# A key load that waits for another load's products: GpSimd's second key transfer held behind w_gate's matmuls

## The chip, the cores and the metric

The kernel runs on one core of one Trainium2 chip. The metric is the device time of one execution in microseconds (us); the median of three runs is compared. All numbers are float32.

## The reference

Two branches read the same x (4 rows of 512) and are mixed by a gate for each row. Branch a is attention of one query per row over a cache of 4096 keys and values in 32 heads of 128; branch b is a gated feed-forward block with 1792 inner columns.

```python
g = sigmoid((x * gate_w).sum(-1, keepdims=True))
q = (x @ wq)                                   # 4 rows x 32 heads x 128
scores = einsum("bhqd,bhkd->bhqk", q, k_cache) * (128 ** -0.5)
a = einsum("bhqk,bhkd->bhqd", softmax(scores), v_cache) @ wo
b = (gelu(x @ w_gate) * (x @ w_up)) @ w_down
out = g * a + (1 - g) * b
```

The caches make up nearly all of the data: 4 x 32 x 4096 x 128 numbers each, 537 MB for the two together. The whole kernel reads 565 MB.

## The kernel before

*Tiles.* The attention runs over 32 tiles (NT). A tile is one row b of x and a group g of four heads, with all 4096 keys: 128 partitions (4 heads x 32), each with 128 keys of 128 numbers, 65,536 bytes to a partition, 8.4 MB for the keys of a tile and as much for its values. Tile i has b = i % 4 and g = i // 4.

*Work of a tile.* DVE multiplies the keys by the query, in place (`products`, L385), and sums over the 128 numbers (`sums`, L391), both in two parts: first the quarter of the tile that shares its place with the neighbouring tile's keys (`shared=True`, 4096 numbers a partition), then the other three quarters (12288). `soft_max` takes the maximum on DVE and the exponentials on ACT. PE multiplies the weights by the values (`pv`, L417), one tile behind. DVE's two big steps make up most of its time.

*Places.* All large operands lie in one on-chip tensor, `big`. Even and odd tiles' keys lie in two places that overlap by one quarter, so the load of key tile i+1 has to wait until DVE has summed the shared quarter of tile i. The values have one place (from `VA` on), so the load of value tile i waits for PE's `pv(i - 1)`. At the start the place of the values is used for other things: first wq, then w_gate (`F0`) and w_up (`F1`), whose places begin where wq lay, and the feed-forward's temporaries.

*Order.* A small planner (`Plan.add`) holds a list of steps. Each step names its engine, what it reads and what it writes, as ranges of named tensors; the planner derives the waits: a step waits for the last earlier step, on another engine, that touches an overlapping range, if one of the two writes it. Each engine runs its own steps in the order of the list. A name in these ranges need not be a tensor: a range of a made-up name makes one step wait for another in the same way. The middle tiles run as a loop over groups with the same steps; tile 0 and the end are written out.

*Loads.* `load` (L260) gives the first four large loads to SyncE's queue (SP): wq, key tile 0, w_gate and w_up. All later ones go to GpSimd's queue (POOL): key tile 1, value tile 0, key tile 2, value tile 1 and so on, in the order of the list. A load issued by GpSimd holds up the ones behind it in that queue while it waits. w_gate and w_up are issued when PE has finished with wq.

*The feed-forward at the start.* In tile 0, between DVE's products of the three quarters and their sums, the list has `gates()` (a tiny product on PE, an Exp on ACT and six small steps on DVE that give the gate), `ffn_up(0)` and `ffn_up(1)` (x times w_gate and x times w_up on PE, 32 matmuls each, L519, and a copy by ACT, L524), `ffn_gelu()` (five steps on DVE with a Tanh on ACT between, L531 to L536, and a transpose into hT, L538) and then the load of value tile 0. The gelu's temporaries lie in w_up's place, so it can begin only when w_up's products are done, and value tile 0's load waits for the last of these steps. The other half of the feed-forward, with w_down, is done at the end, together with the product with wo.

Of the kernel before, what the change touches and what calls it, by code (L numbers as in the profile page):

```python
# [132 lines left out]
def tile_gated_mix(tc: tile.TileContext, x, kc, vc, wq, wo, w_gate, w_up, w_down, gate_w, out):  # L133
# [4 lines left out]
    F = w_gate.shape[1]  # L138
    KC = DM // P
# [5 lines left out]
    NT = B * NG  # L145
    TW = R * D
# [22 lines left out]
    def sb(pool, name, shape):  # L169
        sizes[name] = math.prod(shape[1:])  # L170
        return pool(name, [P] + list(shape[1:]), F32).ap()[:shape[0]]
# [5 lines left out]
    xT = sb(head, "xT", [P, KC, 4, B, 8])  # L177
# [31 lines left out]
    q = sb(ps, "q", [P, B, D])  # L209
# [6 lines left out]
    Q0, F0, F1, W0, D0 = VA, VA, VA + KC * F, VA, VA + TW // 2  # L216
# [4 lines left out]
    def place(a, n):  # L221
        return big[:, a:a + n]

    def z(a, n):
        return ("big", a, a + n)

    def t(*names):
        return [(n, 0, sizes[n]) for n in names]
# [17 lines left out]
    def dve(emit, reads, writes):  # L246
        return add("dve", emit, reads, writes)

    def act(emit, reads, writes):
        return add("act", emit, reads, writes)  # L250

    def pe(emit, reads, writes):
        return add("pe", emit, reads, writes)
# [4 lines left out]
    def load(dst, src, writes, lane):  # L258
        e, queue = ("sp", nc.sync) if sum(x.engine == "sp" for x in plan.steps) < 4 else ("pool", G)
        return add(e, lambda: queue.dma_start(dst, src), (), writes, lane=lane if e == "sp" else "p" + lane, unit=16)  # L260

    def load_kv(kind, i):
        src = (vc, kc)[kind == "k"]
        a = KB_ * (i % 2) if kind == "k" else VA if i < NT - 1 else 0
        s = src[i % B, HT * (i // B):HT * (i // B) + HT].rearrange("h (p r) d -> (h p) (r d)", p=PH)
        load(place(a, TW), s, [z(a, TW)], "vl" if kind == "v" and i == NT - 1 else kind)

    def KA(i):
        return KB_ * (i % 2)
# [86 lines left out]
    def gates():  # L356
        pe(lambda: T.matmul(sm[:, :B], ones[:B], gd, start=True, stop=True), t("ones", "gd"), [("sm", 0, B)])
        act(lambda: A.activation(g4, sm[:, :B], AF.Exp, scale=-1.0), [("sm", 0, B)], t("g4"))
        dve(lambda: V.tensor_scalar(g4, g4, 1.0, None, op0=OP.add), t("g4"), t("g4"))
        dve(lambda: V.reciprocal(g4, g4), t("g4"), t("g4"))  # L360
        dve(lambda: V.tensor_tensor(g16.rearrange("p (j b) -> p j b", b=B), m16.rearrange("p (j b) -> p j b", b=B),
                                    g4[:, None, :].to_broadcast([P, 4, B]), op=OP.mult), t("m16", "g4"), t("g16"))
        dve(lambda: V.tensor_reduce(g1, g16, axis=AX.X, op=OP.add), t("g16"), t("g1"))
        dve(lambda: V.tensor_scalar(half, g1, -0.5, 0.5, op0=OP.mult, op1=OP.add), t("g1"), t("half"))
        dve(lambda: V.tensor_tensor(gmask, g4[:, :, None].to_broadcast([P, B, HT]),
                                    pmask[:, None, :].to_broadcast([P, B, HT]), op=OP.mult), t("g4", "pmask"), t("gmask"))

    def q_pick(g):
        dve(lambda: V.tensor_scalar(HC, hmask[:, bass.ds(row(g - 1) * HT + HT, HT), None].to_broadcast([P, HT, PH]), 1.0,  # L369
                                    None, op0=OP.mult), t("hmask"), t("hc"))  # L370
# [6 lines left out]
    def rows(i, shared):  # L377
        return ((R - RO, R), (0, R - RO))[not shared] if i % 2 == 0 else ((0, RO), (RO, R))[not shared]

    def products(i, shared):  # L380
        b = i % B
        r0, r1 = rows(i, shared)
        k = place(KA(i), TW).rearrange("p (r d) -> p r d", d=D)[:, r0:r1]
        m = [z(KA(i) + r0 * D, (r1 - r0) * D)]
        dve(lambda: V.tensor_tensor(k, k, QB[:, b:b + 1, :].to_broadcast([P, r1 - r0, D]), op=OP.mult),  # L385
            m + t("qb"), m)

    def sums(i, shared):
        r0, r1 = rows(i, shared)
        k = place(KA(i), TW).rearrange("p (r d) -> p r d", d=D)[:, r0:r1]  # L390
        dve(lambda: V.tensor_reduce(SC[i % 2][:, r0:r1], k, axis=AX.X, op=OP.add),  # L391
            [z(KA(i) + r0 * D, (r1 - r0) * D)], [(f"sc{i % 2}", r0, r1)])
# [17 lines left out]
    def pv(i):  # L410
        b, n = i % BP, i // BP % 2
        N, m = RJ * D, R // RJ

        def emit():
            for j in range(m):
                c, m0 = j % 4, PZ + 32 * j - RJ * HT * b
                last = T.matmul(PO[n][32 * c:32 * c + 32].rearrange("p j d -> p (j d)"), PM[:, m0:m0 + 32],  # L417
                                place(VAT(i) + j * N, N), start=b == 0 and j < 4, stop=b == BP - 1 and j >= m - 4)
            return last

        pe(emit, t("PM") + [z(VAT(i), TW)], t(f"po{n}"))

    def gather_a(i):
        n = i // BP % 2
        act(lambda: A.activation(O[n], PO[n], AF.Copy), t(f"po{n}"), t(f"o{n}"))  # L425

    def gather(g):
        N = B // BP

        def emit():  # L430
            for n in range(N):
                m0 = BP * HT * (1 - n)
                for j in range(RJ):
                    T.matmul(sm[:B * HT, :D], selv[:, j, m0:m0 + B * HT], O[n][:, j, :],  # L434
                             start=(n, j) == (0, 0), stop=(n, j) == (N - 1, RJ - 1))
            return T.matmul(sm[:B * HT, D:], RS.rearrange("p b h -> p (b h)"), ones[:, :1], start=True, stop=True)  # L436

        pe(emit, t("o0", "o1", "sel", "RS", "ones"), t("sm"))
# [52 lines left out]
    def attended(w, e):  # L491
        a, m = ES + w * E * 32 + e * 32, (W0, W1)[w] + e * DM
        return place(a, 32), place(m, DM), [z(a, 32), z(m, DM)]
# [21 lines left out]
    def ffn_up(s):  # L515
        def emit():
            for c in range(KC):
                for j in range(4):
                    last = T.matmul(q.rearrange("p b d -> p (b d)")[32 * j:32 * j + 32, :FG], xTf[:, c, :32],  # L519
                                    place((F0, F1)[s] + c * F + j * FG, FG), start=c == 0, stop=c == KC - 1)  # L520
            return last

        pe(emit, t("xT") + [z((F0, F1)[s], KC * F)], t("q"))
        act(lambda: A.activation(fu[:, s, :FG], q.rearrange("p b d -> p (b d)")[:, :FG], AF.Copy),  # L524
            t("q"), [z(FU + s * DM, FG)])

    def ffn_gelu():
        x1, r1 = fu[:, 0, :FG], [z(FU, FG)]
        (t1, z1), (t2, z2), (t3, z3), (th, z4), (y, z5), (v, z6) = (
            (place(F1 + a * DM, FG), [z(F1 + a * DM, FG)]) for a in range(6))  # L530
        dve(lambda: V.tensor_tensor(t1, x1, x1, op=OP.mult), r1, z1)  # L531
        dve(lambda: V.tensor_scalar(t2, t1, 0.044715, 1.0, op0=OP.mult, op1=OP.add), z1, z2)
        dve(lambda: V.tensor_tensor(t3, t2, x1, op=OP.mult), z2 + r1, z3)
        act(lambda: A.activation(th, t3, AF.Tanh, scale=c_gelu), z3, z4)
        dve(lambda: V.scalar_tensor_tensor(y, th, 1.0, x1, op0=OP.add, op1=OP.mult), z4 + r1, z5)  # L535
        dve(lambda: V.scalar_tensor_tensor(v, y, half, fu[:, 1, :FG], op0=OP.mult, op1=OP.mult),  # L536
            z5 + t("half") + [z(FU + DM, FG)], z6)
        dve(lambda: V.transpose(hT, v.rearrange("p (k i) -> p i k", i=FC)), z6, t("hT"))  # L538
# [10 lines left out]
    for i in range(NT):  # L549
        g, b = divmod(i, B)  # L550
        plan.turn = (i - 1) // B if 0 < i < NT - B + 1 else None
        if b == 1 and g + 1 < NG:
            q_pick(g + 1)
        products(i, True)
        sums(i, True)
        if i < NT - 1:
            load_kv("k", i + 1)
        else:
            load_kv("v", i)
        products(i, False)  # L560
        if i == 0:
            gates()
            ffn_up(0)
            ffn_up(1)
            ffn_gelu()
            load_kv("v", 0)
        sums(i, False)
        if i > 0:
            pv(i - 1)
            if i < NT - 1:  # L570
                load_kv("v", i)
            if i % BP == 0:
                gather_a(i - 1)
            if b == 0:
                gather(g - 1)
            if b == 3 and g + 1 < NG:
                q_spread()
        soft_max(i)
        if i > 0 and b == 0:
            weigh(g - 1)  # L580
# [25 lines left out]
    for h in range(2):  # L606
        for e in range(WO_END[1][-1], E):
            s, w, reads = attended(1, e)
# [52 lines left out]
```

## Time and profile before

| what | value |
|---|---|
| median of 3 runs | 1316.59 us (1316.15 to 1318.24) |
| the profiled execution | 1318.02 us, span 1316.6 us |
| mean granted TensorE clock | 0.638 |
| DVE busy | 1158.4 us, 88% of the span |
| PE busy | 354.3 us, 27% |
| ACT busy | 87.3 us, 7% |
| data over the span | 564.8 MB, mean 429 GB/s |
| w_gate's load, issue to landing | 18.2 us |
| w_up's load, issue to landing | 36.8 us |

The profile shows one execution. The span goes from the first to the last instruction; the execution's own time is 1.4 us longer. A row of the timeline gives the start, the duration, the engine with the line and the operation, what it writes and reads, and in brackets how long the engine stood idle before it and what ended that. DMA issues of GpSimd are rows of POOL. A row of a stretch of time gives the length, then each engine's busy time with its number of instructions, the granted clock, the mean busy share of the 16 DMA engines, and the GB/s moved. A packet is counted where it starts, so the share of a short stretch can be over 1.

### The profile page before, as it was taken

The page shows a single profiled execution, that of the slowest core. Times are in us where ns is not written, and L with a number is a line of the kernel's source. Part 1 is how long each engine was busy: PE and PEld are TensorE (multiplying, and loading weights), DVE is VectorE, ACT ScalarE, POOL GpSimd, SP SyncE. Part 2 cuts the span into 40 slices and gives each one's busy share as a digit, 9 for nine tenths or more (in the row PEclk, how much of TensorE's full clock was granted, in tenths as well). Part 3 has the DMA queues.
Part 4 walks back from the last instruction along what each step waited for, and adds up shares of the span by engine and source line. Part 5 has one row for each costly group of instructions (what it writes and reads, how often), then busy time and mean ns, then how long its engine had stood idle before and what let it go on. Part 6 is the DMA issues. An engine that isn't in the chain of part 4 may idle for free.

```text
span 1316.6 us, 6158 instructions
## 1 busy us (share of the span) xinstructions
PE 354.3 (27%) x2512; PEld 100.4 (8%) x2512; DVE 1158.4 (88%) x303; ACT 87.3 (7%) x291; POOL 38.8 (3%) x78
## 2 busy tenths in 40 slices
PE   3212222122332113322211222321133222122227
PEld 0000000000010000100000000100001000010002
DVE  1769999999999898999989899998989999998992
ACT  0000000000000000000000000000000000000001
POOL 0000000000000000000000000000000000000000
PEclk9556665666666566666556666655666665666668
DMA  9988999999999999999999999999999999999998
GB/s 415 443 354 383 445 432 431 442 418 442 440 424 442 434 430 442 424 436 442 422 442 434 430 442 424 436 446 418 442 440 424 442 430 434 442 418 441 438 427 370
DMA packets 10602, 564.83 MB, mean 429 GB/s; under 512 B 1232, under 2 KB 1240, under 8 KB 1504
## 3 DMA queue, kind: packets, MB, share of 16 engines
q0 software_dynamic: 9984, 540.55, 94.9%
q1 hardware_dynamic: 592, 24.13, 4.3%
q8 instruction: 7, 0.11, 0.0%
q14 instruction: 3, 0.02, 0.0%
q10 hardware_dynamic: 16, 0.02, 0.0%
HBM read 564.67 MB, written 0.01 MB: 429 GB/s over the span
## 4 chain that ended last, share of the span: by engine, by line
DMA 71%; DVE 26%; PE 2%; issue 1%; ACT 0%; SPq 0%; DVEq 0%
DMA big<-in_A_k_cache 65%; DVE sc L391 13%; DVE big L385 12%; DMA big<-in_B_w_up 3%; DMA big<-in_A_wo 2%; DMA big<-in_A_wq 2%; PE po L331 1%; PE q L519 0%; PE acc L506 0%; PE wide L498 0%; PE po L506 0%; DVE hT L538 0%; DVE big L536 0%; DVE big L531 0%; DVE big L535 0%
## 5 line engine op out<-in xcount | busy, mean ns | idle before, releaser
L385 DVE TENSOR_TENSOR big<-big,qb 128x4096 f32<-128x4096 f32 x64 | 555.9, 8687 | 86.9 <-DMA big<-in_A_k_cache 86.9
L391 DVE TENSOR_REDUCE sc<-big 128x32 f32<-128x4096 f32 x64 | 555.9, 8686 | 2.3
L417 PE MATMUL po<-big,PM 128*32 128x512 f32 x2048 | 293.8, 738 | 900.0 <-DMA big<-in_A_v_cache 900.0
L417 PEld LDWEIGHTS po<-big,PM 128*32 128x32 f32 x2048 | 72.2, 132 | 1115.7 <-DMA big<-in_A_v_cache 823.6
L403 ACT ACTIVATE PM<-sc,nb 32x128 f32<-32x128 f32 x128 | 67.2, 525 | 478.7 <-DVE nb L398 431.9
L425 ACT ACTIVATE o<-po 128x512 f32<-128x512 f32 x16 | 9.6, 597 | 443.0 <-PE po L417 443.0
L260 POOL DMA_DIRECT2D big<-in_A_v_cache x32 | 16.9, 528 | 607.6 <-PE po L417 560.4
L260 POOL DMA_DIRECT2D big<-in_A_k_cache x31 | 16.5, 532 | 613.2 <-DVE sc L391 613.2
L403 ACT ACTIVATION_READ_ACCUMULATOR PM<-sc,nb 32x1 f32 x128 | 26.1, 204 | 0.0
L375 ACT ACTIVATE qb<-q 128x512 f32<-128x512 f32 x8 | 4.8, 597 | 246.1 <-PE q L373 246.1
L519 PE MATMUL q<-big,xT 128*32 128x448 f32 x64 | 11.4, 883 | 25.3 <-DMA big<-in_B_w_up 13.7
L348 DVE TENSOR_TENSOR big<-po,amask 128x512 f32<-128x512 f32 x2 | 1.3, 686 | 19.0 <-PE po L331 19.0
L434 PE MATMUL sm<-o,sel 128*16 128x128 f32 x128 | 15.4, 273 | 5.8 <-ACT o L425 5.8
L331 PE MATMUL po<-big,xT 128*32 128x512 f32 x64 | 9.4, 755 | 19.1 <-DMA big<-in_A_wq 19.1
L434 PEld LDWEIGHTS sm<-o,sel 128*16 128x16 f32 x128 | 11.7, 97 | 14.4 <-ACT o L425 13.1
L616 DVE COPY res<-acc 4x144 f32<-4x144 f32 x1 | 0.3, 296 | 13.0 <-PE acc L506 13.0
L373 PE MATMUL q<-QM,hc 128*128 128x512 f32 x16 | 10.0, 707 | 4.2 <-DVE hc L369 4.2
L531 DVE TENSOR_TENSOR big<-big 128x448 f32<-128x448 f32 x1 | 0.6, 626 | 10.9 <-PE q L519 10.9
L396 DVE TENSOR_REDUCE m<-sc 128x1 f32<-128x128 f32 x32 | 9.2, 286 | 1.1
L441 DVE RECIPROCAL ri<-sm 16x1 f32<-16x1 f32 x8 | 1.2, 155 | 8.4 <-PE sm L436 8.4
L397 DVE STREAM_TRANSPOSE mt<-m 128x32 f32<-128x32 f32 x32 | 6.8, 212 | 1.1
L398 DVE TENSOR_REDUCE nb<-mt 128x1 f32<-128x32 f32 x32 | 5.9, 186 | 1.1
(78 smaller groups left out, 73.8 us busy)
## 6 DMA issues: line engine op xcount, KB each, us to landing
big<-in_A_wo POOLq DMA_DIRECT2D x1, 4096.0 KB, 28.2
big<-in_B_w_gate SPq DMA_DIRECT2D x1, 3584.0 KB, 18.2
big<-in_B_w_up SPq DMA_DIRECT2D x1, 3584.0 KB, 36.8
big<-in_B_w_down POOLq DMA_DIRECT2D x1, 3584.0 KB, 19.1
big<-in_A_wo POOLq DMA_DIRECT2D x1, 1792.0 KB, 26.3
big<-in_A_wo POOLq DMA_DIRECT2D x1, 1280.0 KB, 28.8
big<-in_A_v_cache POOLq DMA_DIRECT2D x32, 29.1
big<-in_A_wo POOLq DMA_DIRECT2D x1, 512.0 KB, 29.5
```

Source lines behind the costliest of these rows:

```text
L260: return add(e, lambda: queue.dma_start(dst, src), (), writes, lane=lane if e == "sp" else "p" + lane, unit=16)
L331: last = T.matmul(PO[s][32 * j:32 * j + 32].rearrange("p j d -> p (j d)"), xTf[:, c, :32], w[:, n0:n0 + HB * D], start=c == 0, stop=c == K ...
L373: pe(lambda: T.matmul(q.rearrange("p b d -> p (b d)"), HC.rearrange("p h k -> p (h k)"), QM.rearrange("p b d -> p (b d)"), start=True, sto ...
L385: dve(lambda: V.tensor_tensor(k, k, QB[:, b:b + 1, :].to_broadcast([P, r1 - r0, D]), op=OP.mult), m + t("qb"), m)
L391: dve(lambda: V.tensor_reduce(SC[i % 2][:, r0:r1], k, axis=AX.X, op=OP.add), [z(KA(i) + r0 * D, (r1 - r0) * D)], [(f"sc{i % 2}", r0, r1)])
L396: dve(lambda: V.tensor_reduce(M1[n], SC[n], axis=AX.X, op=OP.max), t(f"sc{n}"), t(f"m1{n}"))
L397: dve(lambda: V.transpose(MT, M1[n].to_broadcast([P, PH])), t(f"m1{n}"), t("mt"))
L403: last = A.activation(PM[:, PZ:].rearrange("p (c m) -> p c m", m=32)[s, :, h:RJ * HT:HT], SC[n][s, :].rearrange("p (c j) -> p c j", j=RJ), ...
L417: last = T.matmul(PO[n][32 * c:32 * c + 32].rearrange("p j d -> p (j d)"), PM[:, m0:m0 + 32], place(VAT(i) + j * N, N), start=b == 0 and j ...
L425: act(lambda: A.activation(O[n], PO[n], AF.Copy), t(f"po{n}"), t(f"o{n}"))
L434: T.matmul(sm[:B * HT, :D], selv[:, j, m0:m0 + B * HT], O[n][:, j, :], start=(n, j) == (0, 0), stop=(n, j) == (N - 1, RJ - 1))
L519: last = T.matmul(q.rearrange("p b d -> p (b d)")[32 * j:32 * j + 32, :FG], xTf[:, c, :32], place((F0, F1)[s] + c * F + j * FG, FG), start ...
```

## The change

The load of key tile 1, and no other, gets one more range, `("turn", 0, 1)`, which it is said to write. `ffn_up(s)` is said to read `("turn", s, s + 1)`, so `ffn_up(0)`, the products with w_gate, touches the same range. For the planner to see it first, the call of `ffn_up(0)` moves ahead of the load in the list, and with that ahead of DVE's `products(0, False)` and of `gates()`. As a result GpSimd waits for the last of w_gate's matmuls, besides DVE's sums of the shared quarter, before it issues key tile 1. PE now has w_gate's matmuls ahead of the gate's tiny product, and ACT has w_gate's copy ahead of the gate's Exp. DVE's own order is as before. The number of loads, their sizes, their queues and their order within each queue stay the same. `ffn_up(1)`'s range `("turn", 1, 2)` is touched by no other step.

```diff
@@ load_kv
-        load(place(a, TW), s, [z(a, TW)], "vl" if kind == "v" and i == NT - 1 else kind)
+        load(place(a, TW), s, [z(a, TW)] + [("turn", 0, 1)] * (kind == "k" and i == 1), "vl" if kind == "v" and i == NT - 1 else kind)
@@ ffn_up
-        pe(emit, t("xT") + [z((F0, F1)[s], KC * F)], t("q"))
+        pe(emit, t("xT") + [z((F0, F1)[s], KC * F), ("turn", s, s + 1)], t("q"))
@@ the loop over the tiles
         products(i, True)
         sums(i, True)
+        if i == 0:
+            ffn_up(0)
         if i < NT - 1:
             load_kv("k", i + 1)
         else:
...
         products(i, False)
         if i == 0:
             gates()
-            ffn_up(0)
             ffn_up(1)
             ffn_gelu()
             load_kv("v", 0)
```

## The prediction

> **What bounds the kernel now.** I read the page's DMA queues first, then the span cut into four stretches, then the timeline of the stretch that stood out, and last the start of three loads in tenths of a microsecond. In the queue rows the last figure is the time of the packets as a share of 16 engines' span. In the stretches the last three figures are the granted clock, the DMA share and GB/s.
>
> ```profile
> span 1316.6 us, 6158 instructions
> ...
> PE 354.3 (27%) x2512; PEld 100.4 (8%) x2512; DVE 1158.4 (88%) x303; ACT 87.3 (7%) x291; POOL 38.8 (3%) x78
> ...
> q0 software_dynamic: 9984, 540.55, 94.9%
> q1 hardware_dynamic: 592, 24.13, 4.3%
> ...
> 0.00:77.00 77.00, 24.02 (x136) 7.20 (x136) 33.11 (x38) 3.06 (x5) 1.36 (x7) 0.76 0.99 423
> 77.00:104.75 27.75, 1.74 (x12) 0.43 (x16) 26.83 (x12) 2.69 (x9) 1.06 (x2) 0.54 0.72 303
> 104.75:1310.00 1205.25, 324.34 (x2289) 90.33 (x2284) 1097.93 (x252) 80.44 (x274) 36.38 (x69) 0.63 1.00 434
> 1310.00:1316.60 6.60, 4.25 (x90) 2.41 (x83) 0.56 (x2) 1.14 (x3) 0.00 (x0) 1.00 0.42 169
> ```
>
> The two queues that carry the data fill 99.2% of the span. From 104.75 us to 1310 us the DMA share is 1.00, at 434 GB/s: one unbroken stream, and nothing done earlier by a compute engine can shorten it. The tail after 1310 us is the last products. The only hole is between 77 and 104.75 us: 0.28 x 27.75 us = 7.8 us in which no data moved. DMA is the bound, and what this kernel can win without moving fewer bytes is about 7.8 us. DVE, at 88% of the span, is second. In the hole it is busy nearly all the time (26.83 of 27.75 us), so it is DVE's order of work that left DMA without a load.
>
> ```profile
> 42.28 4.43 DVE L385 TENSOR_TENSOR big<-big,qb 128x4096 f32<-128x4096 f32 x1 [5.73 <-DMA big<-in_A_k_cache]
> 50.79 5.33 PE L519 MATMUL q<-big,xT 128*32 128x448 f32 x32 [11.59 <-DMA big<-in_B_w_gate]
> 51.08 12.95 DVE L385 TENSOR_TENSOR big<-big,qb 128x12288 f32<-128x12288 f32 x1
> 51.48 0.67 POOL L260 DMA_DIRECT2D big<-in_A_k_cache  x1 [48.28 <-DVE sc L391]
> 56.18 0.54 ACT L524 ACTIVATE big<-q 128x448 f32<-128x448 f32 x1 [16.77 <-PE q L519]
> 63.95 0.16 DVE L359 TENSOR_SCALAR g<-g 128x4 f32<-128x4 f32 x1
> ...
> 64.84 0.17 DVE L365 TENSOR_TENSOR gmask<-g,pmask 128x16 f32<-128x16 f32 x1
> 69.84 6.04 PE L519 MATMUL q<-big,xT 128*32 128x448 f32 x32 [13.72 <-DMA big<-in_B_w_up]
> 75.94 0.63 DVE L531 TENSOR_TENSOR big<-big 128x448 f32<-128x448 f32 x1 [10.94 <-PE q L519]
> ...
> 79.68 0.94 DVE L538 STREAM_TRANSPOSE hT<-big 128x448 f32<-128x448 f32 x1
> 80.54 12.91 DVE L391 TENSOR_REDUCE sc<-big 128x96 f32<-128x12288 f32 x1
> 80.93 0.53 POOL L260 DMA_DIRECT2D big<-in_A_v_cache  x1 [28.78 <-DVE hT L538]
> 94.42 4.42 DVE L385 TENSOR_TENSOR big<-big,qb 128x4096 f32<-128x4096 f32 x1
> 103.01 8.68 PE L417 MATMUL po<-big,PM 128*32 128x512 f32 x64 [27.13 <-DMA big<-in_A_v_cache]
> 103.59 0.53 POOL L260 DMA_DIRECT2D big<-in_A_k_cache  x1 [22.13 <-DVE sc L391]
> ...
> big<-in_B_w_gate SPq DMA_DIRECT2D x1, 3584.0 KB, 18.2
> big<-in_B_w_up SPq DMA_DIRECT2D x1, 3584.0 KB, 36.8
> ```
>
> The timeline's columns are start, duration, engine, line and operation; in brackets stands the idle time before it and what ended it. The last two rows are the page's DMA issues, with the time from issue to landing. The start reads like this. Key load 1 is issued at 51.48 us, as soon as DVE's sums of the first quarter free its place, while w_up, queued behind w_gate on SP, is still on its way. The two loads share the engines, so w_up is seen by PE only at 69.84 us, 19.05 us after w_gate, though both hold 3584 KB. DVE idles 10.94 us for w_up's products, does the gelu, and only its last step (hT) frees the place of value load 0, issued at 80.93 us. By then key load 1 is through: hole one. Because DVE is late, key load 2 too is issued late, at 103.59 us, after value load 0 has landed (PE starts on it at 103.01): hole two.
>
> **The change, part by part.** *The wait.* Key load 1 now also waits for the first group of L519, which ends at 50.79 + 5.33 = 56.12 us; with the 0.3 us that GpSimd takes after a release (hT ends at 80.62, its load is issued at 80.93) it goes out at 56.4, 4.9 us later than before. Behind it in GpSimd's queue stands only value load 0, which is due far later. Its reader, DVE's next tile, is due at 94.42 before and about 83.9 after (below).
>
> *w_up alone.* 3.67 MB at 434 GB/s are 8.5 us behind w_gate: PE sees it at 50.79 + 8.5 = 59.3 us instead of 69.84, and its last bytes move between about 58.2 and 59.2. L519's second group takes 6.04 us: 65.3. DVE's small steps for the gate end at 65.01 anyhow, so the gelu starts at 65.4 instead of 75.94: DVE is 10.5 us earlier. The gelu's chain (75.94 to 80.62) ends at 70.1.
>
> *ffn_up(0) ahead of the gate's product.* PE's tiny product for the gate, and ACT's Exp behind it, now stand behind w_gate's group and its copy:
>
> ```profile
> 38.62 0.59 PE L357 MATMUL sm<-gd,ones 4*128 4x4 f32 x2
> ...
> 39.24 0.17 ACT L358 ACTIVATE g<-sm 128x4 f32<-128x4 f32 x1
> ```
>
> They end near 57 us (56.72 for the copy, 0.17 for the Exp) and DVE wants the result at 63.95: 6.9 us of cover, cost nothing. Were the cover gone, the delay would fall on the gelu one for one.
>
> *Hole one.* Value load 0 goes out at 70.4. Key load 1 brings the same bytes behind the same bytes as before, so if the stream does not break around 58 us it ends where it ended, by 77 us. The next load then waits in the queue with 5 us to spare, and the hole is gone.
>
> *Hole two.* DVE's tile 1 moves from 94.42 to 83.9, key load 2 from 103.59 to 93.1, its first bytes to 94.3. Value load 0's bytes (128 partitions of 65,536 bytes, 8.39 MB, 19.3 us at 434 GB/s) now follow at once on key load 1's, from 77.2, 4.9 us sooner than the 82.1 of the row below, and end near 96.5: 2.2 us to spare, hole gone. Value load 1 waits for PE's products on value load 0 (103.01 to 111.69 before, 4.9 us earlier now: 106.8), while key load 2 runs from 96.5 to 115.8. From there every load is issued well inside the one before it, as before.
>
> *The new break.* What no row shows is when key load 1's first bytes move. Three loads from GpSimd bound it:
>
> ```profile
> 55.50:55.60 0.10, 0.10 (x8) 0.00 (x0) 0.10 (x1) 0.00 (x0) 0.00 (x0) 1.00 0.00 0
> 55.60:55.70 0.10, 0.10 (x8) 0.00 (x0) 0.10 (x1) 0.00 (x0) 0.00 (x0) 1.00 1.51 655
> 82.00:82.10 0.10, 0.00 (x0) 0.00 (x0) 0.10 (x1) 0.00 (x0) 0.00 (x0) 0.50 0.00 0
> 82.10:82.20 0.10, 0.00 (x0) 0.00 (x0) 0.10 (x1) 0.00 (x0) 0.00 (x0) 0.50 5.82 1966
> 104.70:104.80 0.10, 0.10 (x8) 0.08 (x4) 0.10 (x1) 0.00 (x0) 0.00 (x0) 0.50 0.00 0
> 104.80:104.90 0.10, 0.10 (x8) 0.10 (x4) 0.10 (x1) 0.00 (x0) 0.00 (x0) 0.50 9.52 3277
> ```
>
> 655 GB/s over 0.1 us is one packet of 65,536 bytes, one partition of keys; w_up's partitions hold 28,672 bytes (3584 KB over 128). Value load 0 and key load 2 found idle engines and moved 1.2 us after their issue. Key load 1 found them full of w_up and moved 4.1 us after its issue (51.48 to 55.6). With 1.2 us it would now be ready at 57.6, before w_up ends: break 0. With 4.1 us it comes at 60.5: at most 60.5 - 58.2 = 2.3 us. I take 0, because another small load shows the same delay behind packets that the engines had already taken on:
>
> ```profile
> 1.34 0.25 ACTq L294 DMA_DIRECT2D big<-in_gate_w  x1
> ...
> 10.53 0.68 DVE L321 TENSOR_TENSOR big<-big 4x512 f32<-4x512 f32 x1 [4.66 <-DMA big<-in_gate_w]
> ```
>
> 8 KB issued at 1.34 us, beside wq's load on another queue, were there at 10.53. So the 4.1 us are most likely a wait behind packets taken on earlier (some three of w_up's, 1.06 us each at 434/16 GB/s), and at 57.6 us each engine has about one left. The Trainium skill (DMA: Bandwidth & Descriptors, Queues, rings and completion order) says that each engine goes round-robin between queues packet by packet; by that key load 1 should have come in by about 53.8, some 1.8 us of its delay would be its own, and the sum would be 6.4 us; no row separates the two.
>
> **The sum.** 7.8 us of holes, less 0 for the break (2.3 at worst), less 0.3 because the engines do not run dry at the same moment and the share is rounded: 7.5 us. The profiled execution took 1318.0 us, 1.4 around its span of 1316.6; after, 1310.5. It stands 1.4 above the median of the three runs (1316.59), so for the median 1309.1.
>
> **The rivals.** *Slow start:* the 4.1 us belong to GpSimd's first load itself. The break is 2.3, the gain 5.2, time 1311.4. For it: the issue took 0.67 us against 0.53 later. Against: gate_w.
>
> *Still mixed:* key load 1, ready at 57.6, slips its 2.4-us packets (65,536 bytes at 434/16) in front of w_up's last ones, twice. w_up comes 4.8 us later, DVE gains 5.7 instead of 10.5, key load 2's first bytes come at 104.8 - 5.7 = 99.1, after 96.5: 2.6 us of hole two stay, gain 4.9, time 1311.7.
>
> *Held behind DVE:* the product of 51.08 to 64.03, two inputs of which lie on chip, keeps GpSimd from setting up the load until it ends. First bytes at 65.2, break 7.0, gain 0.5, time 1316.1: no change. Against it: key load 2 was issued at 103.59 beside a product of the same kind, begun at 103.21, and moved 1.2 us later.
>
> ```profile
> 103.21 12.95 DVE L385 TENSOR_TENSOR big<-big,qb 128x12288 f32<-128x12288 f32 x1
> ```
>
> The Trainium skill (SBUF — State Buffer, Who interferes with whom) has this rule: a DVE instruction with two SBUF inputs and a GpSimd instruction that reads SBUF shut each other out for their whole length; by it 1316.1 would stand if setting up a load reads SBUF. The same section infers that writing descriptors needs only the write side, and with that the row of 104.8 agrees.
>
> *Slower:* that hold lasts until DVE falls idle at 65.0, and the start takes 4.1 us on top: first bytes at 69.1, break 10.9, more than the holes it closes, 1319.7. The point from which the change loses is a first byte after 58.2 + 7.5 = 65.7 us.
>
> *Hidden anyway:* the holes close but the stream gives the time back later. The share of 1.00 over 1205 us leaves no place for that. Time 1316.6.
>
> **How the numbers follow.** Forecast 0.69; slow start 0.12; still mixed 0.04; held behind DVE 0.07; hidden 0.03; slower 0.05. 0.2% (2.6 us) is about what a measurement here tells from no change; the three runs spread over 2.1 us. Faster 0.85, same 0.10, slower 0.05. The range leaves out the last three cases: from 1307.8 (all 7.8 us, and 1 us of the runs' spread below) to 1312.8 (slow start's 1311.4 and 1.4 above).
>
> **What would show it.** Right: key load 1 at about 56.4 us, L519's second group at 59.3, value load 0 at 70.4, key load 2 at 93.1, a DMA share near 1.00 from 77 to 104.75, and the rest 7.5 us earlier. A share well under 1 between 58 and 61 us is the slow start. First key packets after 64 us are the hold behind DVE. L519's second group after 61 us is the mix. Wrong altogether would be a stream with holes after 104.75 us.

## The result, and the profile after

The changed kernel takes 1310.31 us (median of 6 runs, 1309.79 to 1310.83) against 1316.67 us before (6 runs, 1316.13 to 1318.24). The ratio is 0.995, with a 95% interval from 0.9937 to 0.9963: faster by 0.5%. The two profiled executions stand 7.5 us apart, 1318.02 against 1310.50, and so do their spans, 1316.6 against 1309.1. Key load 1 is the kernel's second key load, and the first load of any kind that GpSimd issues.

The stretches of the changed kernel, with the same columns as before:

```profile
0.00:77.00 77.00, 22.23 (x136) 6.71 (x136) 43.30 (x43) 3.61 (x6) 1.90 (x8) 0.79 0.99 421
77.00:104.75 27.75, 5.31 (x36) 1.39 (x40) 27.57 (x8) 2.12 (x8) 0.53 (x1) 0.53 0.98 425
...
104.75:1302.00 1197.25, 320.96 (x2255) 89.47 (x2251) 1086.90 (x252) 80.42 (x274) 36.40 (x69) 0.63 1.00 434
```

The DMA share between 77 and 104.75 us went from 0.72 to 0.98. Counted only as far as they lie inside it, the packets of the trace fill this stretch without a gap. Behind it the stream is as it was, a share of 1.00 at 434 GB/s, only that it ends earlier. The gain lies in that one stretch.

The timeline of the changed kernel:

```profile
50.79 5.31 PE L519 MATMUL q<-big,xT 128*32 128x448 f32 x32 [12.12 <-DMA big<-in_B_w_gate]
51.08 12.95 DVE L385 TENSOR_TENSOR big<-big,qb 128x12288 f32<-128x12288 f32 x1
56.03 0.38 PE L357 MATMUL sm<-gd,ones 4*128 4x4 f32 x2
...
56.77 0.67 POOL L260 DMA_DIRECT2D big<-in_A_k_cache  x1 [53.57 <-PE sm L357]
59.26 4.49 PE L519 MATMUL q<-big,xT 128*32 128x448 f32 x32 [2.85 <-DMA big<-in_B_w_up]
...
64.84 0.17 DVE L365 TENSOR_TENSOR gmask<-g,pmask 128x16 f32<-128x16 f32 x1
64.92 0.62 DVE L531 TENSOR_TENSOR big<-big 128x448 f32<-128x448 f32 x1
...
69.90 0.53 POOL L260 DMA_DIRECT2D big<-in_A_v_cache  x1 [12.46 <-DVE hT L538]
...
83.39 4.42 DVE L385 TENSOR_TENSOR big<-big,qb 128x4096 f32<-128x4096 f32 x1
...
92.56 0.53 POOL L260 DMA_DIRECT2D big<-in_A_k_cache  x1 [22.13 <-DVE sc L391]
99.44 8.74 PE L417 MATMUL po<-big,PM 128*32 128x512 f32 x64 [35.69 <-DMA big<-in_A_v_cache]
```

Key load 1 goes out 5.3 us later than before (56.77 against 51.48), and w_up is seen by PE 10.6 us earlier (59.26 against 69.84). The gelu (L531) follows DVE's gate steps at once; the 10.94 us for which DVE waited are gone. Value load 0 goes out at 69.90 instead of 80.93 and key load 2 at 92.56 instead of 103.59, both 11.0 us earlier. In the rows of a tenth of a microsecond the first packets of keys (655 GB/s for each) show up between 58.1 and 58.2 us, 1.4 us after the issue:

```profile
58.00:58.10 0.10, 0.00 (x0) 0.00 (x0) 0.10 (x1) 0.00 (x0) 0.00 (x0) 1.00 0.01 0
58.10:58.20 0.10, 0.00 (x0) 0.00 (x0) 0.10 (x1) 0.00 (x0) 0.00 (x0) 1.00 3.92 1311
```

### The profile page after: what moved, and what is told of

The parts are those of the page before. It is cut to its first block, busy times and chain, and to the rows that moved or that the text cites. A ratio compares the mean times of both kernels' runs of the same rounds, so it can differ in the third digit from the quotient of the medians.

```text
span 1309.1 us, 6159 instructions
## 1 busy us (share of the span) xinstructions
PE 353.3 (27%) x2512; PEld 100.2 (8%) x2512; DVE 1158.3 (88%) x303; ACT 87.3 (7%) x291; POOL 38.8 (3%) x78
## 4 chain that ended last, share of the span: by engine, by line
DMA 70%; DVE 28%; issue 1%; PE 0%; ACT 0%; SPq 0%; DVEq 0%
DMA big<-in_A_k_cache 68%; DVE big L385 14%; DVE sc L391 13%; DMA big<-in_A_wo 2%; PE acc L506 0%; PE wide L498 0%; PE po L506 0%; DVE hT L538 0%; DVE big L536 0%; DVE big L533 0%; DVE big L535 0%; ACT big L512 0%; DVE m L396 0%; ACT big L534 0%; DVE big L531 0%
## 5 line engine op out<-in xcount | busy, mean ns | idle before, releaser
L519 PE MATMUL q<-big,xT 128*32 128x448 f32 x64 | 9.8, 775 | 15.0 <-DMA big<-in_B_w_gate 12.1
L498 PE MATMUL wide<-big 128*32 128x512 f32 x46 | 5.6, 596 | 1.8 <-DMA big<-in_A_wo 1.8
```

## The experiments

The theory: the kernel is a stream of data, only a hole in it costs time, and each hole costs its own length. The change takes the two holes away by letting w_up come alone. The rivals are named with each experiment. The kernels of one group ran on one chip, each timed in five rounds. The kernel before had medians of 1316.53, 1316.65 and 1316.88 us in the three groups. An edit shifts the lines below it, so L521 or L524 in a variant can be the L519 of the changed kernel.

### The order without the wait

```diff
-        load(place(a, TW), s, [z(a, TW)] + [("turn", 0, 1)] * (kind == "k" and i == 1), ...
+        load(place(a, TW), s, [z(a, TW)], ...
```

> The new order of the list alone: w_gate's products stand ahead of the key load and of the gate's product, but the key load does not wait for them. Theory (the time went with the holes in the data stream): key load 1 goes out at about 51.5 us again, w_up is seen by PE near 69.8, the DMA share from 77 to 104.75 us is near 0.72 again, time 1316.7. Rival (the order on PE and ACT itself helps): 1310.3.

1316.33 us; ratio 0.9999 (0.999 to 1.0008). The timeline:

```profile
51.10 0.67 POOL L260 DMA_DIRECT2D big<-in_A_k_cache  x1 [47.91 <-DVE sc L391]
80.62 0.53 POOL L260 DMA_DIRECT2D big<-in_A_v_cache  x1 [28.85 <-DVE hT L538]
103.29 0.53 POOL L260 DMA_DIRECT2D big<-in_A_k_cache  x1 [22.13 <-DVE sc L391]
...
69.81 5.77 PE L519 MATMUL q<-big,xT 128*32 128x448 f32 x32 [13.85 <-DMA big<-in_B_w_up]
```

With the new order and no wait, w_up is late again (69.81) and everything behind it too. The new order alone gains nothing; the gain came with the wait. The share from 77 to 104.75 us was 0.80 where 0.72 was expected, though the span was the same: a fixed stretch of packets counted at their starts is a rough measure of a hole. By the packets themselves the engines stood idle for 6.9 us here and 7.5 us in the first profile of before.

### The wait made longer

Here key load 1 waits for w_up's products too. The gate's product and its Exp go ahead of both groups; `gates_rest` holds the six DVE steps of the gate, which stay where they were, so that DVE's order stays.

```diff
-[("turn", 0, 1)] * (kind == "k" and i == 1)
+[("turn", 0, 2)] * (kind == "k" and i == 1)
...
         if i == 0:
+            gates()
             ffn_up(0)
+            ffn_up(1)
...
         if i == 0:
-            gates()
-            ffn_up(1)
+            gates_rest()
```

> Key load 1 waits for w_up's products too, so it goes out only when PE has ended the second group of L519, near 63.8 us in the changed kernel. Theory (a break in the stream costs its own length): issue near 64.1, first bytes 1.4 later as in the changed kernel (56.77 to 58.15), so 65.5; w_up's bytes end near 58.4; break 7.1 us; nothing else moves enough to matter; time 1310.3 + 7.1 = 1317.4. Rival (what pays is that w_up comes alone, and a later key load is covered by DVE's work): DVE is as early as in the changed kernel, time 1310.3.

1318.01 us; ratio 1.0012 (1.0003 to 1.0021), slower than before. Its timeline and its stretches:

```profile
58.98 4.91 PE L521 MATMUL q<-big,xT 128*32 128x448 f32 x32 [2.31 <-DMA big<-in_B_w_up]
...
64.56 0.67 POOL L260 DMA_DIRECT2D big<-in_A_k_cache  x1 [61.36 <-DVE g L365]
69.61 0.53 POOL L260 DMA_DIRECT2D big<-in_A_v_cache  x1 [4.38 <-DVE hT L540]
86.85 4.43 DVE L387 TENSOR_TENSOR big<-big,qb 128x4096 f32<-128x4096 f32 x1 [3.66 <-DMA big<-in_A_k_cache]
...
96.02 0.53 POOL L260 DMA_DIRECT2D big<-in_A_k_cache  x1 [25.88 <-DVE sc L393]
```

```profile
58.00:65.90 7.90, 4.91 (x32) 1.59 (x32) 7.70 (x10) 0.54 (x1) 0.67 (x1) 0.78 0.01 2
66.00:104.75 38.75, 0.00 (x0) 0.00 (x0) 34.20 (x12) 2.68 (x9) 1.06 (x2) 0.51 0.99 425
...
65.80:65.90 0.10, 0.00 (x0) 0.00 (x0) 0.10 (x1) 0.00 (x0) 0.00 (x0) 1.00 0.00 0
65.90:66.00 0.10, 0.00 (x0) 0.00 (x0) 0.10 (x1) 0.00 (x0) 0.00 (x0) 1.00 9.95 3277
```

w_up comes as early as in the changed kernel (58.98), DVE does its gelu as early, value load 0 goes out as early, and yet the kernel is 7.9 us slower than the changed one (1310.07 in this group). The old holes are closed (0.99 from 66 us on), and a new one stands ahead of them: from 58 us to the keys' first bytes at 65.9 the share is 0.01. By the packets, the engines stood idle for 7.7 us. DVE's early start is worth nothing by itself here; an unbroken stream is what pays. The forecast put the point from which the change loses at a first byte after 65.7 us, so 65.9 should have cost 0.2 us against the kernel before; it cost 1.5. That point was reckoned with holes of 7.5 us, as in one execution of before, while the medians of before and changed stand 6.4 us apart.

### The wait made shorter

w_gate's products become two steps of 16 matmuls, and only the first touches the range that key load 1 waits for.

```diff
-        pe(emit, t("xT") + [z((F0, F1)[s], KC * F), ("turn", s, s + 1)], t("q"))
+        for h in range(2):
+            pe(lambda h=h: emit(range(2 * h, 2 * h + 2)),
+               t("xT") + [z((F0, F1)[s], KC * F)] + [("turn", s, s + 1)] * (h == 0), t("q"))
```

> Key load 1 waits for the first half of w_gate's products only, about 2.3 us less than in the changed kernel: issue near 54.2, ready near 55.5 us, when each engine still has about three of w_up's packets (1.06 us each) to move. Theory A (engines have taken on some three packets ahead, so a load on another queue comes behind these): key packets start near 58.1 all the same, w_up is seen near 59.3, time 1310.3. Theory B (engines change between the queues after every packet): key packets from about 56.5, two of them (2.4 us each) in front of w_up's last ones, w_up seen near 64, DVE 4 to 5 us later, key load 2 after the end of value load 0 by some 1.5 us, time 1311.8.

1309.82 us; ratio 0.9949 (0.9935 to 0.9962). The timeline, then the tenths of a microsecond:

```profile
54.67 0.67 POOL L260 DMA_DIRECT2D big<-in_A_k_cache  x1 [51.48 <-PE q L519]
...
59.27 5.96 PE L519 MATMUL q<-big,xT 128*32 128x448 f32 x32 [3.08 <-DMA big<-in_B_w_up]
```

```profile
57.90:58.00 0.10, 0.00 (x0) 0.00 (x0) 0.10 (x1) 0.00 (x0) 0.00 (x0) 1.00 0.00 0
58.00:58.10 0.10, 0.00 (x0) 0.00 (x0) 0.10 (x1) 0.00 (x0) 0.00 (x0) 0.60 3.03 1311
```

Issued 2.1 us earlier than in the changed kernel, the keys start at nearly the same moment, 58.0, and w_up is seen at the same moment, 59.27. With 1.2 to 1.4 us from issue to first bytes, as in the other loads, the load was ready by about 56; it then came in some 2 us later, behind the last two of w_up's packets of 1.06 us on each engine. For the start of the keys theory A holds and theory B does not. A load issued at 51.48 comes too early to be covered by this, one issued at 54.67 came late enough for w_up's data.

It was not late enough for w_up's landing each time. A second profile of this kernel, from the last group below, has the issue at 54.51 and the keys again at 58.1, but this row for w_up:

```profile
61.58 6.09 PE L519 MATMUL q<-big,xT 128*32 128x448 f32 x32 [5.89 <-DMA big<-in_B_w_up]
```

w_up's data had moved by 58.7 us there as well. But behind the data each of the 16 engines moves one packet of 4 bytes on SP's queue, and PE starts 0.4 to 0.6 us after the last of these in this kernel's two profiles and in the first ones of before and changed. In this execution six of the 16 came only at 60.8 to 61.1 us, each behind a key packet of 2.4 us. DVE was 2.4 us later for it; value load 0 went out at 72.72, still before key load 1 had ended. So the shorter wait is close to being too short. The four profiles with the change's own wait (three of the changed kernel, one with DVE made late) have w_up seen between 59.12 and 59.26.

### One queue instead of a wait

The kernel before, with key load 1 in SP's queue behind w_up, but for a piece of 256 KB (two small steps on DVE that wait for the load are not shown):

```diff
+        if kind == "k" and i == 1:
+            m = RJ * D
+            add("sp", lambda: nc.sync.dma_start(place(a + m, TW - m), s[:, m:]), (), [z(a + m, TW - m)], lane="k1", unit=16)
+            load(place(a, m), s[:, :m], [z(a, m)], kind)
+            return
```

> The kernel before, but key load 1 (all but its first 512 numbers of each partition, which stay on GpSimd) goes into SP's queue, behind w_up in the same queue, at its old time of about 51.5 us; no wait for w_gate's products. DVE gets two tiny steps at the end of tile 0 that wait for this load. Theory (what w_up suffered from was a second queue beside its own, not the early issue): w_up is seen near 59.3 to 60, the hole from 77 us on is gone, time 1310. Rival (a key load issued at 51.5 us delays w_up whatever queue it is in): w_up near 70, time 1316.7.

1309.63 us; ratio 0.9945 (0.9931 to 0.9958). The timeline and the stretch:

```profile
51.06 0.33 SPq L268 DMA_DIRECT2D big<-in_A_k_cache  x1
51.34 0.68 POOL L260 DMA_DIRECT2D big<-in_A_k_cache  x1 [48.15 <-DVE sc L396]
...
60.85 5.34 PE L524 MATMUL q<-big,xT 128*32 128x448 f32 x32 [4.87 <-DMA big<-in_B_w_up]
```

```profile
77.00:104.75 27.75, 5.98 (x40) 1.58 (x44) 27.49 (x10) 2.13 (x8) 0.53 (x1) 0.54 1.03 443
```

Issued at its old time, the load no longer delays w_up, since it comes behind it in the same queue; that w_up is still 1.6 us later than in the changed kernel, and later than the 60 us expected, fits the small piece on the other queue. The early issue was not the fault. The fault was the load's place on a second queue, from which the engines took packets in turn with w_up's: in the trace of before, the starts of w_up's packets and of the keys' follow each other in alternating bursts from 55.7 us on. Whether any second queue would do this, or only GpSimd's, was not tried.

### DVE made late

The changed kernel with two sums of 4.42 us done twice over on DVE ahead of the sums of tile 0.

```diff
+        if i == 0:
+            for _ in range(2):
+                dve(lambda: V.tensor_reduce(SC[0][:, :RO], ..., axis=AX.X, op=OP.add),
+                    [z(KA(0), RO * D)], [("sc0", 0, RO)])
         sums(i, False)
```

> The changed kernel with two sums over 4096 numbers a partition done once more on DVE (4.42 us each, 8.9 us together, the same numbers written again) between hT and the sums of tile 0. Value load 0 is issued at its time, but key load 2 goes out at 92.6 + 8.9 = 101.5 us, first bytes at 102.7. The engines ran out of value load 0 from 97.0 on (spread to 98.5). Theory: only the part of DVE's delay past the end of the stream costs: about 102.7 - 97.6 = 5.1 us, time 1315.4. Rivals: DVE is 88% busy and takes all of it up later, 1310.3; or DVE is the bound at the start and all of it is lost, 1319.2.

1315.85 us; ratio 0.9998 (0.9989 to 1.0007). The timeline and the stretches:

```profile
69.79 0.53 POOL L260 DMA_DIRECT2D big<-in_A_v_cache  x1 [13.02 <-DVE hT L538]
101.36 0.53 POOL L260 DMA_DIRECT2D big<-in_A_k_cache  x1 [31.03 <-DVE sc L391]
```

```profile
77.00:82.00 5.00, 0.00 (x0) 0.00 (x0) 4.97 (x2) 0.00 (x0) 0.00 (x0) 0.50 1.03 446
...
96.50:103.00 6.50, 2.35 (x12) 0.60 (x16) 6.47 (x3) 0.00 (x0) 0.53 (x1) 0.50 0.40 132
```

Hole one stays closed and hole two is back, 4.8 us by the packets. 8.8 us more on DVE cost 5.5 us against the changed kernel (1310.31, on another chip), 0.4 more than expected: DVE's delay costs what of it goes past the end of value load 0, and the 3 us before that are free. Neither of the rivals, nothing or all of it, is near.

### The kernel before, a second profile

> The kernel before, unchanged, for a second profile. If its profiled execution takes about 1316.7 us and its holes between 77 and 104.75 us add up to some 6.5 us, the difference of 1.1 us between the gain of the profiles (7.5) and that of the medians (6.4) lies in the holes of the first profile. If the holes are 7.8 us again, it lies elsewhere in the execution.

1316.75 us; ratio 0.9999 (0.999 to 1.0008). This time the profiled execution took 1315.83 us, with a span of 1314.4:

```profile
78.95 0.53 POOL L260 DMA_DIRECT2D big<-in_A_v_cache  x1 [26.91 <-DVE hT L538]
101.61 0.53 POOL L260 DMA_DIRECT2D big<-in_A_k_cache  x1 [22.13 <-DVE sc L391]
...
68.78 5.12 PE L519 MATMUL q<-big,xT 128*32 128x448 f32 x32 [12.47 <-DMA big<-in_B_w_up]
```

Here w_up is seen 1.06 us earlier than in the first profile (68.78 against 69.84), its matmuls take 0.92 us less (5.12 against 6.04), and key load 2 goes out 1.98 us earlier. The span is 2.2 us shorter. In all kernels with a hole ahead of key load 2 the span is that load's issue plus a constant: 1316.6 - 103.59 = 1213.0 in the first profile of before, 1213.2 with the order alone (span 1316.5), 1213.1 with DVE made late (span 1314.5), 1212.8 here. The share from 77 to 104.75 us was 0.83, or 4.7 us without data where some 6.5 were expected; but the execution was also 0.9 us shorter than the 1316.7 that went with the 6.5.

Packets counted only as far as they lie inside a stretch give a better measure. The idle time of the 16 engines between 50 and 110 us, in the mean of one engine and to within about 0.1 us, is this:

| profiled execution | its time | engines idle | time less idle |
|---|---|---|---|
| before, first | 1318.02 us | 7.5 us | 1310.5 us |
| before, second | 1315.83 us | 5.3 us | 1310.5 us |
| the order alone | 1317.95 us | 6.9 us | 1311.0 us |
| the longer wait | 1317.85 us | 7.7 us | 1310.1 us |
| DVE made late | 1315.85 us | 4.9 us | 1310.9 us |
| changed, first | 1310.50 us | 0.0 us | 1310.5 us |
| changed, second | 1310.83 us | 0.1 us | 1310.7 us |

Executions that lie 7.5 us apart come to within 0.9 us of each other once their holes are taken off. The five profiles that are not in the table, one of the changed kernel and four of its variants, have at most 0.2 us idle and took 1309.31 to 1310.73 us. The two of before differ by 2.2 us in time and by 2.2 us in their holes, nearly all of it in hole one (4.8 against 2.7 us). So the size of the holes differs from execution to execution, and the first profile had large ones. That accounts for the gap between the 7.5 us of the profiles and the 6.4 of the medians; the executions that were only timed have no trace to show it in each.

### The changed kernel again, and the variants side by side

> The changed kernel once more, on the same chip as the three others: 1310.3 us, about 6.4 us below the kernel before by the medians, with no hole from 58 to 105 us. If the difference here is 7.5, as between the two profiled executions, the 1.1 us between profile and medians was spread of the runs; if it is 6.4 again, the profiled execution of before was one of its slower ones.

1310.07 us (5 runs, 1309.65 to 1310.84) against 1316.53 before: 6.5 us; ratio 0.9951 (0.9938 to 0.9965). The medians of the two groups say 6.4 to 6.5 us.

In a group of their own, the changed kernel and the two variants:

> The changed kernel beside its two variants on one chip. Theory: its first key packets start on idle engines and run slower than later ones, and there is a break of up to 0.2 us, together some 0.5 us that the variants do not have. 1310.1 us.

> The key load that waits for half of w_gate's products. Theory: ready before w_up ends, no break, 1309.8 us. Rival: no difference from the changed kernel.

> The key load in SP's queue behind w_up, without the wait. Theory: key packets follow w_up's in the same queue, no break and no slow first packets, 1309.6 us. Rival: no difference from the changed kernel, 1310.1.

1310.37 us (ratio 0.9949, 0.9935 to 0.9963), 1310.19 us (0.9955, 0.9942 to 0.9969) and 1310.63 us (0.9951, 0.9938 to 0.9965). The half microsecond that the theory gave the variants does not show in the medians: the order of the three turned round between the groups. These runs do not tell the shorter wait, the one queue and the change as it is apart. Two of the five runs of the shorter wait, 1311.96 and 1312.61 us, lie above every run of the changed kernel; neither was profiled.

## Why the prediction was right, and where it was off

*DMA is the bound, and only the stretch from 77 to 104.75 us can be won.* Right. The share there rose to 0.98, nothing changed after it, and two kernels in which DVE was as early as in the changed one (the longer wait: 7.9 us more for 7.7 us of holes) or later (DVE made late: 5.5 us more for 4.9) took the time of their holes within a microsecond.

*The wait.* Key load 1 was forecast for 56.4 and went out at 56.77. The term that was too small is the 0.3 us after a release: from the end of the matmuls it took 0.67 us. The profile names the gate's small product (L357, ended at 56.41) as the releaser, but it is not the cause: in the longer wait, where no such product follows the matmuls, the issue at 64.56 also stood 0.67 us behind their end (63.89). Why this wait takes longer than the one on DVE is open; the 0.4 us lay under w_up's bytes.

*w_up alone.* Forecast for 59.3 us, seen at 59.26.

*Value load 0 and key load 2.* Forecast for 70.4 and 93.1, issued at 69.90 and 92.56. The half microsecond is PE's second group, which took 4.49 us where the row of before had 6.04, so the gelu no longer waited for it at all. That size was luck of the execution: in the second profile of the changed kernel the group took 5.98 us, and value load 0 went out at 70.15.

*The new break.* The forecast took 0 with 2.3 us as the worst. Keys moved at 58.1, 1.4 us after their issue, as w_up ended; by the packets the break was 0.1 to 0.3 us in the three profiles of the changed kernel. With that the slow start falls: the same load, GpSimd's first, needed 4.1 us before and 1.4 now, so most of the 4.1 us were not its own. The shorter wait fits what the forecast took them for, w_up's packets taken on ahead. The Trainium skill (DMA: Bandwidth & Descriptors, Queues, rings and completion order) has the engines change between queues after every packet. The first packets of a load differ from that rule, and the measurement decides: in the shorter wait the keys stood some 2 us, two packets, behind w_up. The alternating bursts that follow in the trace of before agree with it. The forecast's sum by that rule, 6.4 us, should by its own terms be 6.3 (ready at 59.4 against 58.2: a break of 1.2). That the medians also stand 6.4 us apart is a coincidence, since no profile of the changed kernel has a break near 1.2 us.

*Held behind DVE.* Did not happen. The issue at 56.77 stood in the middle of DVE's product of 51.08 to 64.03, and the keys moved at 58.1. The Trainium skill (SBUF — State Buffer, Who interferes with whom) infers that writing descriptors needs the write side, which such a product leaves free; the 1.4 us agree. With it falls *Slower*, whose 1319.7 takes off 7.8 us for the closed holes where the other rivals take off 7.5.

*Still mixed.* Did not happen; w_up came at 59.26. Part of it did in one profile of the shorter wait, where w_up's landing, though not its data, came behind a key packet.

*The size.* The forecast for the profiled execution was 1310.5, and it took 1310.50; that it agrees to the last digit is luck, since the 16 runs of the changed kernel spread over 1.2 us. For the median it was 1309.1 against 1310.31, inside the range. The step that failed is the last line of the sum: it took the holes of an execution that stood 1.4 us above the median off the median itself. That execution was slow because its holes were large, so the two were not independent; the second profile of before, 2.2 us shorter, has 2.2 us less of holes. Taken off its own time, 1318.0 - 7.5, the sum was right for a kernel without holes, whose runs then lie close together.

## What to carry to other kernels

Where the DMA share stays at 1.00 for nearly the whole span, look for the stretches where it does not: without moving fewer bytes, their length is about all that can be won. In this kernel each microsecond of hole closed was close to a microsecond won, and an earlier DVE without a closed hole won nothing. A large load issued early on a second queue can be the cause of such a hole, because the engines take its packets in turn with those of a small load that somebody needs first. Put it behind the small one, with a wait or in the same queue, but have it ready before the small one ends, since a break made there costs its full length. And take a gain read from one execution off that execution's time, not off a median, when the stall it removes is what makes that execution slow.

## What the runs showed of the hardware

A load issued beside another queue's stream moved its first bytes 4.1 us after its issue at 51.48 us, 3.3 at 54.67 and 1.4 at 56.77, where other loads needed 1.2 us on idle engines. That it came in behind packets already taken on fits: two or three of w_up's packets of 1.06 us account for the first two. After that the queues shared, and w_up, alone done by 59.3 us, came at 68.8 to 69.8. A load can also have all its data in place and be seen late: w_up's data had moved by 58.7 us in one profile of the shorter wait, and PE saw it at 61.58, because six engines moved a key packet ahead of the 4 bytes that follow the data.

The time at which a load shared by two queues lands varied by 1.06 us between two executions of the same kernel (68.78 and 69.84), and PE's 32 matmuls behind it by 0.92 us (5.12 and 6.04). Together, 1.98 us, they account for nearly all of the 2.2 us between the two spans. The changed kernel's 16 runs lie between 1309.65 and 1310.84 us, while those of before reach from 1315.09 to 1318.7. In the seven profiled executions of the table above, the time less the holes lies within 0.9 us; that the holes also make the spread of the runs without a profile fits, but was not tried by itself.
